# Keys and queries of four attention units turned by TensorE instead of by small transfers

## The chip, the cores and the metric

The kernel runs on one core of one Trainium2 chip. Time is device microseconds (us) of one execution on that core. Three executions of the kernel before took 579.68, 582.94 and 583.62 us; their median is 582.94 us. One more execution was taken by the hardware profiler; the rows shown here come from it.

## The reference

Three layers follow each other. Everything is float32, and the matrix products are made as sums of three products of a rounded part and a remainder, so that they keep float32's precision.

```
q, k, v: (2, 8, 768, 64)                   # batch, heads, tokens, head size
state = gamma[h] * state + k[t] v[t]^T     # retention, token by token, per head
y[t]  = q[t] state / sqrt(64)
x = y as (1536 tokens, 512)
h = x @ w_in   (512 x 2048);  g = max(h, 0) + log1p(exp(-|h|));  x = g @ w_out   (2048 x 512)
h = x @ w2_in  (512 x 2048);  g = h * clip(h + 3, 0, 6) / 6;     out = g @ w2_out (2048 x 512)
```

## The kernel before, in words

**Attention** is made in 12 units of 128 tokens (`attend(u)`), chunked: with q, k and v of a unit in SBUF, TensorE makes S (scores, from the turned `kT` and `qT`), I (scores times values), D (the unit's k-v product, added to the state `st`), and C (the carried state times `qT`). ScalarE then copies the unit's output from PSUM to `x`. Units 0 to 3 are whole units of 128 tokens; from unit 4 on (`START`) a unit is two halves of 64, and its PSUM banks are banks 2 and 3 alone (`bank_groups`): the turned keys, the turned queries, the scores and the outputs of these units take the same two banks after each other. Units 0 to 7 turn q and k on TensorE (T: 4 transposes of 128x128 each for k and for q against `ident`); ScalarE copies kT from PSUM, VectorE multiplies qT from PSUM by a table. Units 8 to 11 (`FIRST` on) fetch q and k a second time, in blocks (`kb`, `qb`: per unit 32 transfers of 16 KB, issued from SP's and POOL's queues), which VectorE's 32x32 transpose turns in SBUF.

**The first MLP layer** works on three chunks of 512 tokens, and on 16 column tiles of w_in and 16 row tiles of w_out. A G1 (`gemm1`) is 12 matmuls of 128x512 for one tile of w_in, a G2 (`gemm2`) 12 for one tile of w_out. Chunk 0 is made plainly while the attention units 4 to 11 stand in the gaps between its G1 and G2. Chunks 1 and 2 are made together: for `PLAIN` pairs of tiles plainly (4 G1 a pair over both chunks), for the other pairs (`PAIRS`) by seven products instead of eight (`early_step`, products P1 to P7 of 6 matmuls each, 42 where the plain way has 48), whose operands are sums and differences of x (`xl`) and of the words of w_in (`forms`, from words kept in DRAM as `words_in` and fetched back into `wf`). Every weight tile arrives as 64-bit words (`raw`) and is turned into float32 (`cv`) by ScalarE and VectorE (`Words.made`): ScalarE writes the low bits and the sign, then either VectorE scales and caps (two instructions) or ScalarE scales and VectorE clamps (one each, `BY_ACT`).

**The second MLP layer** works on two blocks of 768 tokens (b = 0 is block A) and 8 pairs of tiles, in 16 steps of seven products (`xf`, 128x384) and 12 sums (`w,parts`, 128x512) each. Stage 0 is block A with pairs 0 to 3, stage 1 block B with all eight pairs, stage 2 block A with pairs 4 to 7. `operands(b)` makes the seven x operands `xf` of a block from `between` (the first layer's result, which stays in SBUF) by 7 copies on ScalarE and 7 + 4 subtractions on VectorE. Those of block A are stored to DRAM (`stash_xP`) after stage 0 and fetched again for stage 2. The words of this layer are made from `late_in` and `late_out` at times that are set against the step that uses them.

**Order.** The kernel adds tasks with a cost, a due time and the buffers they take and give; `Plan.run` simulates the engines with these costs and records the instructions of all engines in the order it finds. TensorE's due times come from the written list `pe`: the attention blocks are put into it by `spread(units, start, per)`, one block each `per` GEMMs.

Of the kernel before, what the change touches and what calls it, by code (L numbers as in the profile page):

```python
# [18 lines left out]
P = 128  # L19
# [125 lines left out]
def kernel(ctx, tc, q, k, v, w1_in, w1_out, w2_in, w2_out, table, out):  # L145
# [28 lines left out]
    def BY_DVE(n):  # L174
# [2 lines left out]
    BY_DMA = ()  # L177

    def BY_ACT(n):
        return n >= 20  # L180

    def DIRECT(n):
        return True
# [62 lines left out]
    room("hi", 2, [P, CH], F32R)  # L246
    room("lo", 3, [P, CH], F32R)
    for name, n, shape, dtype in (("sums", 1, [P, 4, CH // 2], F32), ("wf", 1, [P, 2, CH], F32), ("xl", 7, [P, 2, 2, CH], F32R), ("hs", 3, [P, CH], F32), ("g2", 5, [P, CH], F32), ("hi2", 7, [P, CH], F32R), ("lo2", 7, [P, CH], F32R),
                                  ("basel", 1, [P, CH], F32), ("partl", 2, [P, CH], F32), ("totall", 1, [P, CH], F32), ("xf", 7, [P, 2, 2, QT], F32R), ("keep", START + 2, [P, CH], F32), ("tf0", 2, [P, 2, QT], F32), ("tf1", 2, [P, 2, QT], F32),
                                  ("base", 1, [P, QT], F32), ("part", 2, [P, QT], F32), ("total", 1, [P, QT], F32),  # L250
                                  ("c", 2, [P, 2, QT], F32), ("ob", 4, [P, CH], F32), ("e2", 2, [P, 2, QT], F32), ("parts", 3, [P, 2, 2, QT], F32R)):
        nc.pool(name, n)
        slots[name], kinds[name] = {}, (shape, dtype)
# [23 lines left out]
        pe += [("S", u)] + [("C", u)] * (u % (S // P) > 0) + [("D", u)] + ([("Tk", u + 1), ("Tq", u + 1)] if u + 1 < START else []) + [("I", u)]  # L277
    gaps = {}

    def spread(units, start, per):  # L280
        for n, u in enumerate(units):
            todo = ("T", "S", "I", "C")[u >= FIRST:]
            for i, block in enumerate(todo):
                gaps.setdefault(start + int((len(todo) * n + i) * per), []).extend({"T": [("Tk", u), ("Tq", u)], "I": [("I", u), ("D", u)]}.get(block, [(block, u)]))
# [251 lines left out]
    for i, key in enumerate(order):  # L536
# [3 lines left out]
    shapes = {n: [P, H, D] for n in ("q", "k", "v", "vs")}  # L540
    shapes.update({n: [P, NP, C] for n in ("kT", "qT", "pt", "kb", "qb")})
    counts = ({"q": LD, "k": LD, "v": LD, "kT": 1, "qT": 2, "vs": 2},
              {"kb": 1, "qb": 1, "k": 2, "v": 2, "kT": 1, "qT": 1, "vs": 1, "pt": 1})
# [58 lines left out]
    def attend(u):  # L602
# [37 lines left out]
        if u < START:  # L640
            at = [begin + 10 * u, begin + 10 * u + 1, begin + 10 * u + 3]
        else:
            at = [d["S" if ph else "Tk"] - 9.0 + x / 2 for x in range(3)]
        ik, iv = load("k", at[0], 2 if u == 0 else 1), load("v", at[2])
        if ph:
            ikb, iqb = (task("SP", 0.48 * 4 * (SHARE[n] + 1), blocks(n), [], d["S"] - 25.0, take=own(n), load=2.0, hold=HOLD + d["S"] - 30.0) for n in ("kb", "qb"))
        else:
            iq = load("q", at[1])
        if u == START - 1:
            for f in order[AHEAD:]:  # L650
# [17 lines left out]
        if ph:  # L668
            kt = task("DVE", TT, in_blocks("kb", "kT"), [ikb], d["S"] - 2.5, take=own("kT"), give=[("kb", u)])
            qt = task("DVE", TT, in_blocks("qb", "qT"), [iqb], d["S"] - 1.8, take=own("qT"), give=[("qb", u)])  # L670
            qt = task("DVE", TT, lambda: nc.vector.tensor_tensor(tile_of("qT"), tile_of("qT"), tq_sb, ALU.mult), [qt, ready["q"]], d["S"] - 1.1)
        else:
            tp = task("PE", cost["Tk"], turned("k"), [ik, ready.get(("o", u - 1)) if u > START else None], d["Tk"], take=[("bank", ("kP", u))])
            kt = task("ACT", ACP, lambda: nc.scalar.activation(tile_of("kT"), bank(("kP", u)), AF.Copy), [tp], d["S"] - 1.0,
                      take=own("kT"), give=[("kP", u)])
            tp = task("PE", cost["Tq"], turned("q"), [iq], d["Tq"], take=[("bank", ("qP", u))], give=[("q", u)])
# [316 lines left out]

    B_OF = {"P1": (0, 0), "P2": (1, 0), "P3": (1, 1), "P4": 4, "P5": 1, "P6": 2, "P7": 3}

    def operands(b):


        i = b * MID
        x = lambda j, k: x2(b)[:, 2 * j:2 * j + 2, k * QT:(k + 1) * QT]  # L1000
        before = T["x2", b]
        when = {name: due[name, i] - (30.0 if b == 0 else 5.0) for name in PRODUCTS}
        made = {}
        early = HOLD + due["P1", i] - 45.0 + 21.0 * b

        def tf(n):
            return at_slot((f"tf{b}", n))

        def put(n, a, c, op, after, at):
            made[n] = nc.add("DVE", dve(2 * QT), lambda: nc.vector.tensor_tensor(tf(n), a(), c(), op), after, at, take=[(f"tf{b}", (f"tf{b}", n))], hold=early)  # L1010

        put(1, lambda: x(0, 1), lambda: x(0, 0), ALU.subtract, before, when["P6"] - 2.5)
        put(2, lambda: x(1, 1), lambda: tf(1), ALU.subtract, [made[1]], when["P6"] - 1.5)
        put(3, lambda: x(1, 1), lambda: x(0, 1), ALU.subtract, before, when["P7"] - 1.5)
        put(4, lambda: x(1, 0), lambda: tf(2), ALU.subtract, [made[2]], when["P4"] - 1.5)
        users = {1: [made[2]], 2: [made[4]]}
        for n, us in users.items():
            for u in us:
                u.give.append((f"tf{b}", n))
                nc.users.setdefault((f"tf{b}", n), []).append(u)  # L1020
        for name in PRODUCTS:
            n, key = B_OF[name], ("xf", b, name)
            source = (lambda n=n: tf(n)) if isinstance(n, int) else (lambda n=n: x(*n))
            give = [(f"tf{b}", n)] if isinstance(n, int) else []
# [8 lines left out]
            c = nc.add("SP", 0.45, lambda key=key, home=home: nc.sync.dma_start(out=home, in_=at_slot(key).rearrange("p a j n -> p (a j n)").bitcast(F32)),  # L1033
                       [a, d], when[name] + 4.0, give=[key], load=2.4)
            again = "xf", 2, name
            i = len(STEPS) - (NPAIR - MID)
            T["xf", 2, name] = [nc.add("SP", 0.45, lambda key=again, home=home: nc.sync.dma_start(out=at_slot(key).rearrange("p a j n -> p (a j n)").bitcast(F32), in_=home),
                                       [c], due[name, i] - 8.0, take=[("xf", again)], load=2.4, hold=HOLD + due[name, i] - 20.0)]
# [170 lines left out]
```

## Time and profile before

| | |
|---|---|
| median of three executions | 582.94 us (579.68 to 583.62) |
| profiled execution, its own time | 581.4 us |
| its span in the profile | 579.6 us |
| TensorE (PE) busy | 561.5 us |
| VectorE (DVE) busy | 430.4 us |
| ScalarE (ACT) busy | 358.0 us |
| GpSimd (POOL) busy | 33.7 us |
| moved by DMA | 112.60 MB |
| granted TensorE clock | 1.00 in every stretch |

The span is what the profile's rows cover; the profiled execution's own time is 1.8 us longer, and 1.5 us below the median of the other three. Matmuls are pipelined, so a row's duration is longer than the distance to the next matmul's start.

### The profile page before, as it was taken

The page shows a single profiled execution, that of the slowest core. Times are in us where ns is not written, and L with a number is a line of the kernel's source. Part 1 is how long each engine was busy: PE and PEld are TensorE (multiplying, and loading weights), DVE is VectorE, ACT ScalarE, POOL GpSimd, SP SyncE. Part 2 cuts the span into 40 slices and gives each one's busy share as a digit, 9 for nine tenths or more (in the row PEclk, how much of TensorE's full clock was granted, in tenths as well). Part 3 has the DMA queues.
Part 4 walks back from the last instruction along what each step waited for, and adds up shares of the span by engine and source line. Part 5 has one row for each costly group of instructions (what it writes and reads, how often), then busy time and mean ns, then how long its engine had stood idle before and what let it go on. Part 6 is the DMA issues. An engine that isn't in the chain of part 4 may idle for free.

```text
span 579.6 us, 9697 instructions
## 1 busy us (share of the span) xinstructions
PE 561.5 (97%) x3667; PEld 476.6 (82%) x3667; DVE 430.4 (74%) x768; ACT 358.0 (62%) x578; POOL 33.7 (6%) x61
## 2 busy tenths in 40 slices
PE   8999999899899999999999999999999999999997
PEld 7777887677688888887888888888888989888995
DVE  4999997886796786979996678754988884445434
ACT  3589969888494546476974774538779862232220
POOL 0000532423000000000000000000000000000000
PEclk9999999999999999999999999999999999999999
DMA  9999796967862316199899351152746742955003
GB/s 198 232 292 290 218 251 138 314 169 207 271 246 77 105 72 220 72 297 323 299 414 329 134 182 37 42 163 103 284 158 235 285 146 81 379 203 190 1 1 110
DMA packets 91088, 112.60 MB, mean 194 GB/s; under 512 B 49312, under 2 KB 66720, under 8 KB 91040
## 3 DMA queue, kind: packets, MB, share of 16 engines
q1 hardware_dynamic: 88784, 109.87, 58.2%
q0 software_dynamic: 2256, 2.10, 1.8%
q8 instruction: 29, 0.48, 0.3%
q14 instruction: 19, 0.16, 0.1%
HBM read 82.06 MB, written 28.57 MB: 191 GB/s over the span
## 4 chain that ended last, share of the span: by engine, by line
PE 75%; DMA 9%; ACT 7%; DVE 5%; issue 1%; SPq 1%; DVEq 0%; POOL 0%; ACTq 0%; POOLq 0%
PE banks L45 75%; DMA raw<-in_moe_w_out_dram 4%; ACT cv L45 2%; DMA stash_out<-raw 1%; DMA kb<-in_k_dram 1%; ACT raw L45 1%; ACT w L45 1%; SPq L45 1%; DMA stash_h<-hs 1%; DMA g<-stash_h 1%; DVE raw L45 1%; DMA qb<-in_q_dram 1%; DVE cv L45 1%; ACT e L45 1%; ACT parts L45 1%
## 5 line engine op out<-in xcount | busy, mean ns | idle before, releaser
L45 PE MATMUL banks<-w,parts 128*128 128x512 f32 x579 | 137.0, 390 | 0.0
L45 PE MATMUL banks<-xf,w 128*128 128x384 f32 x672 | 125.4, 338 | 2.4 <-ACT base L45 1.5
L45 PEld LDWEIGHTS banks<-w,parts 128*128 128x128 f32 x579 | 108.0, 188 | 21.2
L45 PE MATMUL banks<-hi,w 128*128 128x512 f32 x384 | 125.2, 393 | 0.0
L45 PEld LDWEIGHTS banks<-xf,w 128*128 128x128 f32 x672 | 117.8, 188 | 8.3 <-ACT base L45 2.7
L45 PEld LDWEIGHTS banks<-hi,w 128*128 128x128 f32 x384 | 72.1, 188 | 15.3
L45 PE MATMUL banks<-xl,w 128*128 128x512 f32 x348 | 82.5, 391 | 0.4 <-DVE hs L45 0.4
L45 PEld LDWEIGHTS banks<-xl,w 128*128 128x128 f32 x348 | 64.9, 188 | 14.7 <-DVE hs L45 0.8
L45 PE MATMUL banks<-lo,w 128*128 128x512 f32 x192 | 75.0, 391 | 0.9 <-DVE lo L45 0.9
L45 ACT ACTIVATE e<-c,three 128x384 f32<-128x384 f32 (+1 forms) x32 | 24.6, 770 | 54.4 <-DVE c L45 54.1
L45 ACT ACTIVATE cv<-raw,half 128x512 uint32<-128x512 uint32 x64 | 48.3, 755 | 9.2 <-DMA raw<-in_moe_w_in_dram 4.3
L45 ACT ACTIVATE cv<-raw 128x512 f16<-128x512 int32 x64 | 50.6, 790 | 1.4
L45 DVE TENSOR_SCALAR raw<-raw 128x512 f32<-128x512 f32 x84 | 35.7, 426 | 15.6 <-ACT raw L45 13.2
L45 DVE SCALAR_TENSOR_TENSOR cv<-raw,cv 128x512 uint32<-128x512 uint32 x64 | 44.2, 690 | 1.5
L45 PE MATMUL banks<-x_hi,w 128*128 128x512 f32 x128 | 42.9, 401 | 2.1 <-ACT g L45 1.3
L45 ACT ACTIVATE hi<-g 128x512 fp32r<-128x512 f32 x48 | 30.0, 627 | 21.1 <-DVE g L45 12.4
L45 PEld LDWEIGHTS banks<-lo,w 128*128 128x128 f32 x192 | 36.1, 188 | 8.5 <-DVE lo L45 1.2
L45 DVE TENSOR_TENSOR parts<-c,parts 128x768 fp32r<-128x768 f32 x32 | 30.6, 957 | 14.2 <-ACT parts L45 13.9
L45 ACT ACTIVATE e<-e 128x512 f32<-128x512 f32 x48 | 29.6, 627 | 18.2 <-DVE e L45 18.0
L45 DVE TENSOR_TENSOR lo<-g,hi 128x512 fp32r<-128x512 f32 x48 | 32.9, 687 | 8.1 <-ACT hi L45 7.4
L45 ACT ACTIVATE parts<-c 128x768 fp32r<-128x768 f32 x32 | 27.0, 844 | 17.3 <-DVE c L45 17.2
L45 DVE TENSOR_TENSOR c<-total,banks 128x384 f32<-128x384 f32 x16 | 8.8, 553 | 36.1 <-PE banks L45 36.0
(102 smaller groups left out, 689.5 us busy)
## 6 DMA issues: line engine op xcount, KB each, us to landing
raw<-in_moe_w_in_dram SPq DMA_DIRECT2D x32, 512.0 KB, 5.4
raw<-in_moe_w_out_dram SPq DMA_DIRECT2D x32, 512.0 KB, 6.1
w<-stash_out SPq DMA_DIRECT2D x32, 512.0 KB, 5.3
w<-parts_out SPq DMA_DIRECT2D x16, 512.0 KB, 7.1
stash_out<-raw SPq DMA_DIRECT2D x16, 512.0 KB, 3.0
stash_xP<-xf SPq DMA_DIRECT2D x7, 768.0 KB, 7.0
xf<-stash_xP SPq DMA_DIRECT2D x7, 768.0 KB, 8.4
parts_out<-w SPq DMA_DIRECT2D x8, 512.0 KB, 6.4
```

The costliest lines, as they stand in the source:

```text
L45: return self.plan.tc.keep_in_program_order(getattr(self.engine, op)(*args, **kwargs))
```

## The change

Units 8 to 11 no longer fetch q and k in blocks: they turn q and k on TensorE as units 4 to 7 do (`TURNED = 'kq'`), with kT copied by ScalarE and qT multiplied from PSUM by VectorE. Their blocks are spread one each 1.2 GEMMs instead of 1.5, with T in front. `PLAIN` goes from 2 to 1, so chunks 1 and 2 have seven pairs made by products and one plain. `BY_ACT` starts at tile 16 instead of 20, so four more tiles of the first layer are scaled by ScalarE. Block A's operands of stage 2 are made again from `between` (`operands(stage)` for three stages) instead of stored and fetched. The due times of the second layer's words are 4 us later, their fetches may start 8 us earlier.

```
-    PLAIN = 2
+    PLAIN = 1
+    TURNED = 'kq'
     def BY_ACT(n):
-        return n >= 20
+        return n >= 16
...
+    def turns(u):
+        return "kq" if u < FIRST else TURNED
     def spread(units, start, per):
         for n, u in enumerate(units):
-            todo = ("T", "S", "I", "C")[u >= FIRST:]
+            todo = ("T", "S", "I", "C")[not turns(u):]
...
-    spread(range(FIRST, NU), 18, 1.5)
+    spread(range(FIRST, NU), 18, 1.2)
...  in late_out
-        at = due["P1", USED[f // 2]] - (40 - 2.0 * f if f < 2 * MID else 20)
-        t = x.made(at, at - 10.0, 1.45, [], hold=(HOLD + at - 24) * (f >= 2 * MID))
+        at = due["P1", USED[f // 2]] - (40 - 2.0 * f if f < 2 * MID else 16)
+        t = x.made(at, at - 10.0, 1.45, [], hold=(HOLD + at - 36) * (f >= 2 * MID))
...  in late_in
-        at = due["P1", USED[p]] - (20 if p else 12)
+        at = due["P1", USED[p]] - (16 if p else 12)
...  in attend
         if ph:
-            ikb, iqb = (task("SP", 0.48 * 4 * (SHARE[n] + 1), blocks(n), [], ...) for n in ("kb", "qb"))
-        else:
+            ib = {n[0]: task(...) for n in ("kb", "qb") if n[0] not in TURNED}
+        if "q" in turns(u):
             iq = load("q", at[1])
...
-            kt = task("DVE", TT, in_blocks("kb", "kT"), [ikb], d["S"] - 2.5, take=own("kT"), give=[("kb", u)])
-            qt = task("DVE", TT, in_blocks("qb", "qT"), [iqb], d["S"] - 1.8, take=own("qT"), give=[("qb", u)])
-            qt = task("DVE", TT, lambda: nc.vector.tensor_tensor(tile_of("qT"), tile_of("qT"), tq_sb, ALU.mult), ...)
...  now for units 8 to 11 too:
             tp = task("PE", cost["Tk"], turned("k"), [ik, ready.get(("o", u - 1)) if u > START else None], ..., take=[("bank", ("kP", u))])
             kt = task("ACT", ACP, lambda: nc.scalar.activation(tile_of("kT"), bank(("kP", u)), AF.Copy), [tp], ...)
+            tp = task("PE", cost["Tq"], turned("q"), [iq, ready.get(("o", u - 1)) if u >= FIRST else None], ..., take=[("bank", ("qP", u))], give=[("q", u)])
             qt = task("DVE", PSX, lambda: nc.vector.tensor_tensor(tile_of("qT"), bank(("qP", u)), tq_sb, ALU.mult), ...)
...
-    def operands(b):
-        i = b * MID
+    def operands(stage):
+        i, b = STAGE.index(stage), stage % 2
...
-            T["xf", b, name] = [a, d]
-            if b:
-                continue
-            home = kept(f"stash_x{name}", 4 * QT)
-            ...  store of xf to home, and its fetch for stage 2
+            T["xf", stage, name] = [a, d]
...
-    for b in range(2):
-        operands(b)
+    for stage in range(3):
+        operands(stage)
```

How the instructions move is shown at three places. The first is TensorE at unit 11, the last one: `ident,k` and `ident,q` are the transposes, `qT,kT` is S, `pt,vs` is I, `vs,k` is D, `xl` rows are a plain G1 of chunk 1, `hi` and `lo` rows belong to a G2. Before:

```order
L45 MATMUL banks<-hi_95,w_1786 128x512
L45 MATMUL banks<-qT_0_151,kT_0_150 64x64 x16
L45 MATMUL banks<-xl_1373,w_1461 128x512 x6
L45 MATMUL banks<-xl_1377,w_1461 128x512 x6
L45 MATMUL banks<-pt_0_153,vs_0_152 64x64 x16
L45 MATMUL banks<-vs_0_152,k_1_147 64x64 x8
L45 MATMUL banks<-hi_96,w_89 128x512
```

and now:

```order
L45 MATMUL banks<-hi_95,w_88 128x512
L45 MATMUL banks<-ident,k_1_149 128x128 x4
L45 MATMUL banks<-ident,q_1_147 128x128 x4
L45 MATMUL banks<-xl_1631,w_1530 128x512 x6
L45 MATMUL banks<-xl_1651,w_1530 128x512 x6
L45 MATMUL banks<-qT_0_153,kT_0_152 64x64 x16
L45 MATMUL banks<-hi_96,w_1368 128x512
```

The transposes stand one GEMM ahead of S. The same holds at units 8 to 10.

The second place is ScalarE from unit 8's output copy (`x_190<-banks`) to unit 9's kT copy in the changed kernel; `cv` and `raw` rows make words of the first layer, `g`, `e`, `hi` belong to the activation:

```order
L45 ACTIVATE hi_95<-g_93 128x512
L45 ACTIVATE raw_0_69<-raw_0_69 128x512
L45 ACTIVATE x_190<-banks 128x2x4x64
L45 ACTIVATE cv_1_75<-raw_1_70,half 128x512
L45 ACTIVATE w_1416<-cv_3_77 128x512
L45 ACTIVATE cv_1_75<-raw_1_70 128x512
L45 ACTIVATE raw_1_70<-raw_1_70 128x512
L45 ACTIVATE g_92<-banks 128x512
L45 ACTIVATE kT_0_152<-banks 128x512
L45 ACTIVATE e_90<-e_90 128x512
```

The kT copy is new there; five instructions stand between it and the output copy, which frees the banks that the transposes take.

The third place is VectorE at unit 9 before, where a transpose of a block (`kT<-kb`) stands among the first layer's work:

```order
L45 TENSOR_SCALAR raw_1_70<-raw_1_70 128x512
L45 SCALAR_TENSOR_TENSOR cv_3_77<-raw_1_70,cv_3_77 128x512
L45 TENSOR_SCALAR e_91<-g_93 128x512
L45 TENSOR_TENSOR w_82<-cv_3_77,w_82 128x512
L45 STREAM_TRANSPOSE kT_0_150<-kb_0_144 128x512
L45 TENSOR_TENSOR pt_0_153<-banks,small 128x2x4x64
L45 TENSOR_SCALAR raw_2_71<-raw_2_71 128x512
```

and now:

```order
L45 TENSOR_TENSOR w_1416<-cv_3_77,w_1416 128x512
L45 TENSOR_SCALAR raw_1_70<-raw_1_70 128x512
L45 TENSOR_TENSOR qT_0_153<-banks,tq_sb 128x512
L45 SCALAR_TENSOR_TENSOR cv_1_75<-raw_1_70,cv_1_75 128x512
L45 SCALAR_TENSOR_TENSOR g_94<-g_94,e_90 128x512
```

No instruction of VectorE waits for a block transfer any more; one multiplication from PSUM is left of three instructions.

## Rows read from the trace of the kernel before

**Rows 1.** The page, section 1: busy us, share of the span, instructions.
```profile
PE 561.5 (97%) x3667; PEld 476.6 (82%) x3667; DVE 430.4 (74%) x768; ACT 358.0 (62%) x578; POOL 33.7 (6%) x61
```
**Rows 2.** Windows: stretch, length, busy PE, PEld, DVE, ACT, POOL, clock, DMA, GB/s.
```profile
32.00:100.00 68.00, 68.00 (x749) 54.37 (x740) 62.89 (x124) 60.63 (x101) 16.97 (x27) 1.00 0.85 235
100.00:151.00 51.00, 44.07 (x532) 34.06 (x528) 40.20 (x73) 39.72 (x66) 15.69 (x26) 1.00 0.79 221
151.00:260.00 109.00, 109.00 (x562) 89.61 (x552) 85.42 (x152) 66.18 (x109) 0.00 (x0) 1.00 0.50 171
260.00:310.00 50.00, 49.63 (x219) 40.66 (x218) 48.88 (x87) 38.95 (x69) 0.00 (x0) 1.00 0.92 339
...
400.00:450.00 50.00, 48.76 (x241) 43.03 (x240) 41.44 (x76) 41.15 (x67) 0.00 (x0) 1.00 0.59 208
...
490.00:580.00 90.00, 85.44 (x426) 76.49 (x424) 38.34 (x60) 22.52 (x33) 0.00 (x0) 1.00 0.41 150
```
**Rows 3.** Timeline, PE, 100 to 151: start, us, instructions, [idle before, releaser].
```profile
105.39 0.68 PE L45 MATMUL banks<-qT,st 64*64 64x64 f32 x16 [0.98 <-DVE st L45]
106.33 0.68 PE L45 MATMUL banks<-qT,st 64*64 64x64 f32 x16 [0.25 <-DVE st L45]
...
113.41 0.69 PE L45 MATMUL banks<-qT,kT 64*64 64x64 f32 x32 [0.71 <-DVE qT L45]
...
123.74 1.15 PE L45 MATMUL banks<-qT,st 64*64 64x64 f32 x32
...
129.17 0.50 PE L45 MATMUL banks<-x_hi,w 128*128 128x512 f32 x1 [1.33 <-ACT g L45]
...
136.96 0.73 PE L45 MATMUL banks<-x_hi,w 128*128 128x512 f32 x2 [0.75 <-DMA w<-cv]
...
143.50 1.15 PE L45 MATMUL banks<-qT,st 64*64 64x64 f32 x32
...
146.01 0.50 PE L45 MATMUL banks<-lo,w 128*128 128x512 f32 x1 [0.93 <-DVE lo L45]
...
150.50 0.69 PE L45 MATMUL banks<-qT,kT 64*64 64x64 f32 x32 [1.71 <-DVE qT L45]
```
**Rows 4.** Timeline, DVE, unit 11's keys.
```profile
144.67 0.71 DVE L45 STREAM_TRANSPOSE kT<-kb 128x512 f32<-128x512 f32 x1 [3.05 <-DMA qb<-in_q_dram]
```
**Rows 5.** Timeline, PE, unit 5's transposes between a G2 and a G1.
```profile
43.08 0.60 PE L45 MATMUL banks<-ident,k 128*128 128x128 f32 x4
43.51 0.60 PE L45 MATMUL banks<-ident,q 128*128 128x128 f32 x4
43.87 0.48 PE L45 MATMUL banks<-x_hi,w 128*128 128x512 f32 x1
...
46.69 0.39 PE L45 MATMUL banks<-hi,w 128*128 128x512 f32 x1
```
**Rows 6.** Timeline, PE, a run of products of chunks 1 and 2.
```profile
183.84 16.48 PE L45 MATMUL banks<-xl,w 128*128 128x512 f32 x72
```
**Rows 7.** Timeline, ACT, the output copies of units 8, 9 and 10.
```profile
109.53 0.58 ACT L45 ACTIVATE x<-banks 128x512 f32<-128x512 f32 x1
...
127.54 0.58 ACT L45 ACTIVATE x<-banks 128x512 f32<-128x512 f32 x1
...
147.93 0.58 ACT L45 ACTIVATE x<-banks 128x512 f32<-128x512 f32 x1
```
**Rows 8.** Groups by form: count, busy us, mean ns of one, idle before.
```profile
L45 DVE TENSOR_TENSOR w<-sums,w 128x512 fp32r<-128x512 f32 x28 | 18.4, 685 | 0.7 <-ACT w L45 0.7
...
L45 DVE TENSOR_TENSOR xf<-tf,xf 128x768 fp32r<-128x768 f32 x8 | 7.6, 953 | 0.3 <-ACT xf L45 0.3
...
L45 ACT ACTIVATE xf<-tf 128x768 fp32r<-128x768 f32 x8 | 6.7, 840 | 5.3 <-PE banks L45 4.2 <-DVE tf L45 0.8
...
L45 DVE TENSOR_TENSOR sums<-wf 128x256 f32<-128x256 f32 x12 | 4.7, 420 | 2.5 <-DMA wf<-words_in 2.5
```
**Rows 9.** Timeline, PE, hand-over from stage 0 to stage 1.
```profile
363.55 2.41 PE L45 MATMUL banks<-xf,w 128*128 128x384 f32 x12 [0.27 <-ACT base L45]
```

More of the change, by code (lines that the diff above doesn't have):

```diff
@@ L278 @@
     gaps = {}
+    def turns(u):
+        return "kq" if u < FIRST else TURNED
     def spread(units, start, per):
         for n, u in enumerate(units):
-            todo = ("T", "S", "I", "C")[u >= FIRST:]
+            todo = ("T", "S", "I", "C")[not turns(u):]
             for i, block in enumerate(todo):
-                gaps.setdefault(start + int((len(todo) * n + i) * per), []).extend({"T": [("Tk", u), ("Tq", u)], "I": [("I", u), ("D", u)]}.get(block, [(block, u)]))
+                gaps.setdefault(start + int((len(todo) * n + i) * per), []).extend({"T": [("T" + n, u) for n in turns(u)], "I": [("I", u), ("D", u)]}.get(block, [(block, u)]))
     spread(range(START, FIRST), 0, 1.2)
-    spread(range(FIRST, NU), 18, 1.5)
+    spread(range(FIRST, NU), 18, 1.2)
     n = 0
@@ L467, in late_in @@
         x = [Words(1, (1, 0, 2 * p + f), words[1][0]) for f in range(2)]
-        at = due["P1", USED[p]] - (20 if p else 12)
-        t = [v.made(at + 2 * f, at - 10.0 + f, 1.75, [v.raw_k], hold=(HOLD + at - 24) * (p >= MID)) for f, v in enumerate(x)]
+        at = due["P1", USED[p]] - (16 if p else 12)
+        t = [v.made(at + 2 * f, at - 10.0 + f, 1.75, [v.raw_k], hold=(HOLD + at - 36) * (p >= MID)) for f, v in enumerate(x)]
         forms(1, p, lambda f: x[f].w().bitcast(F32), t, [v.cv_k for v in x], at)
@@ L542 @@
     counts = ({"q": LD, "k": LD, "v": LD, "kT": 1, "qT": 2, "vs": 2},
[L543 removed]
+              {"q": 2, "k": 2, "v": 2, "kT": 1, "qT": 1, "vs": 1, "pt": 1})
     for n, m in counts[0].items():
@@ L642, in attend @@
         else:
-            at = [d["S" if ph else "Tk"] - 9.0 + x / 2 for x in range(3)]
+            at = [d["T" + turns(u)[0] if turns(u) else "S"] - 9.0 + x / 2 for x in range(3)]
         ik, iv = load("k", at[0], 2 if u == 0 else 1), load("v", at[2])
         if ph:
-            ikb, iqb = (task("SP", 0.48 * 4 * (SHARE[n] + 1), blocks(n), [], d["S"] - 25.0, take=own(n), load=2.0, hold=HOLD + d["S"] - 30.0) for n in ("kb", "qb"))
-        else:
+            ib = {n[0]: task("SP", 0.75 * 4 * (SHARE[n] + 1), blocks(n), [], d["S"] - 25.0, take=own(n), load=2.0, hold=HOLD + d["S"] - 30.0) for n in ("kb", "qb") if n[0] not in TURNED}
+        if "q" in turns(u):
             iq = load("q", at[1])
@@ L667, in attend @@
         sc, ds, o = ([(n, j, u) for j in range(2)] for n in ("sc", "ds", "o"))
-        if ph:
-            kt = task("DVE", TT, in_blocks("kb", "kT"), [ikb], d["S"] - 2.5, take=own("kT"), give=[("kb", u)])
-            qt = task("DVE", TT, in_blocks("qb", "qT"), [iqb], d["S"] - 1.8, take=own("qT"), give=[("qb", u)])
-            qt = task("DVE", TT, lambda: nc.vector.tensor_tensor(tile_of("qT"), tile_of("qT"), tq_sb, ALU.mult), [qt, ready["q"]], d["S"] - 1.1)
+        if "k" not in turns(u):
+            kt = task("DVE", TT, in_blocks("kb", "kT"), [ib["k"]], d["S"] - 2.5, take=own("kT"), give=[("kb", u)])
         else:
@@ L675, in attend @@
                       take=own("kT"), give=[("kP", u)])
-            tp = task("PE", cost["Tq"], turned("q"), [iq], d["Tq"], take=[("bank", ("qP", u))], give=[("q", u)])
+        if "q" not in turns(u):
+            qt = task("DVE", TT, in_blocks("qb", "qT"), [ib["q"]], d["S"] - 1.8, take=own("qT"), give=[("qb", u)])
+            qt = task("DVE", TT, lambda: nc.vector.tensor_tensor(tile_of("qT"), tile_of("qT"), tq_sb, ALU.mult), [qt, ready["q"]], d["S"] - 1.1)
+        else:
+            tp = task("PE", cost["Tq"], turned("q"), [iq, ready.get(("o", u - 1)) if u >= FIRST else None], d["Tq"], take=[("bank", ("qP", u))], give=[("q", u)])
             qt = task("DVE", PSX, lambda: nc.vector.tensor_tensor(tile_of("qT"), bank(("qP", u)), tq_sb, ALU.mult), [tp, ready["q"]],
@@ L994 @@
     B_OF = {"P1": (0, 0), "P2": (1, 0), "P3": (1, 1), "P4": 4, "P5": 1, "P6": 2, "P7": 3}
-    def operands(b):
-        i = b * MID
+    def operands(stage):
+        i, b = STAGE.index(stage), stage % 2
         x = lambda j, k: x2(b)[:, 2 * j:2 * j + 2, k * QT:(k + 1) * QT]
         before = T["x2", b]
-        when = {name: due[name, i] - (30.0 if b == 0 else 5.0) for name in PRODUCTS}
+        when = {name: due[name, i] - (5.0 if stage else 30.0) for name in PRODUCTS}
         made = {}
-        early = HOLD + due["P1", i] - 45.0 + 21.0 * b
+        early = HOLD + due["P1", i] - (24.0 if stage else 45.0)
         def tf(n):
-            return at_slot((f"tf{b}", n))
+            return at_slot((f"tf{stage}", n))
         def put(n, a, c, op, after, at):
-            made[n] = nc.add("DVE", dve(2 * QT), lambda: nc.vector.tensor_tensor(tf(n), a(), c(), op), after, at, take=[(f"tf{b}", (f"tf{b}", n))], hold=early)
+            made[n] = nc.add("DVE", dve(2 * QT), lambda: nc.vector.tensor_tensor(tf(n), a(), c(), op), after, at, take=[(f"tf{stage}", (f"tf{stage}", n))], hold=early)
         put(1, lambda: x(0, 1), lambda: x(0, 0), ALU.subtract, before, when["P6"] - 2.5)
@@ L1018, in operands @@
             for u in us:
-                u.give.append((f"tf{b}", n))
-                nc.users.setdefault((f"tf{b}", n), []).append(u)
+                u.give.append((f"tf{stage}", n))
+                nc.users.setdefault((f"tf{stage}", n), []).append(u)
         for name in PRODUCTS:
-            n, key = B_OF[name], ("xf", b, name)
+            n, key = B_OF[name], ("xf", stage, name)
             source = (lambda n=n: tf(n)) if isinstance(n, int) else (lambda n=n: x(*n))
-            give = [(f"tf{b}", n)] if isinstance(n, int) else []
+            give = [(f"tf{stage}", n)] if isinstance(n, int) else []
             a = nc.add("ACT", act(2 * QT), lambda key=key, source=source: nc.scalar.activation(at_slot(key)[:, 0], source(), AF.Copy),
@@ L1028, in operands @@
                 at_slot(key)[:, 1], source(), at_slot(key)[:, 0].bitcast(F32), ALU.subtract), [a], when[name] + 0.9, give=give)
-            T["xf", b, name] = [a, d]
-            if b:
-                continue
-            home = kept(f"stash_x{name}", 4 * QT)
[L1033 to L1038, printed above, removed]
+            T["xf", stage, name] = [a, d]
     def step(i):
```

2 lines of the change are left out of this document (1 added, 1 removed).

## Prediction, made before the changed kernel ran

> **What bounds the kernel.** I read the engine table first, then the stretches, then the timeline of TensorE. TensorE is busy 561.5 of 579.6 us [rows 1], at full clock in every stretch shown [rows 2]. So the time is TensorE's work plus its waits, and only 18.1 us are not work. Most of that is at the two ends or in one place: from 100 to 151 us it works 44.07 of 51.00 us, 6.93 us idle [rows 2]. From 32 to 100 and from 151 to 260 it never stops; 400 to 450 loses 1.24 us, and most of the 4.56 us lost after 490 are the end, when the last tile is scaled and stored. The changed attention units 8 to 11 stand in the stretch from 100 to 151, so the reader should see there who keeps TensorE waiting. The timeline names it [rows 3]: S of units 9 and 11 waits for qT, 0.71 and 1.71 us; C of unit 8 waits for the state, 0.98 and 0.25 us; a G2 waits for `lo`, 0.93 us; one G1 for a bank that ScalarE frees late, 1.33 us; another for weights that POOL's queue brings, 0.75 us. These make 6.66 of the 6.93 us.
>
> Behind several of them is one thing. VectorE works in order, and its transpose of unit 11's keys sat 3.05 us until a block had landed [rows 4]; `lo` at 146.01 and qT at 150.50 stood behind it. The same engine makes the words that ScalarE needs next.
>
> **TensorE's own work.** Unit 5 shows what turning costs: its 8 transposes begin at 43.08 and the next GEMM at 43.87, so 0.79 us; that GEMM takes 2.82 us to the next one's start [rows 5], where 12 matmuls in a run take 12 x 0.2266 = 2.72 us (16.48 us less the last one's overlap of 0.39, over 71 steps [rows 6]). So 0.89 us a unit, and 4 x 0.89 = **+3.56 us**. The lower bound is 4 x 0.79 = 3.16. The Trainium skill, in "VectorE: DVE Perf Modes", section "The three transpose paths", gives 390 ns for a 128x128 transpose on TensorE (in bf16) and 311 ns for VectorE's 32x32 blocks. By that figure, an estimate, 32 transposes would cost 12.5 us of the binding engine. The trace speaks against that sum: eight in 0.79 us.
>
> The seventh pair made by products takes 42 matmuls instead of 48: 6 x 0.2266 = **-1.36 us**. The 14 transfers of `stash_xP` never kept TensorE waiting in a row here, so taking them away is worth nothing by itself.
>
> **The waits in 100 to 151.** The two qT waits and `lo` go with the blocks: 3.35 us. C of unit 8 came right behind D; now a GEMM of 2.72 us stands between, more than its 1.23 us: gone for units 8 to 10, and unit 11 keeps six matmuls, 1.36 us. The remaining 2.35 us hang on ScalarE and POOL. POOL issued 48 of the block transfers, and ScalarE was late because words were late; I count these as gone too: **-6.93 us**. If they stay, it is -4.58.
>
> New waits can come, since all these units share PSUM banks 2 and 3. T of unit 9 cannot begin until unit 8's output has been copied out, and S waits for the new kT copy (0.59 us, four of them) on ScalarE. In the trace the output copies of units 8, 9 and 10 end at 110.11, 128.12 and 148.51 [rows 7], and their C ended at 107.01, 124.89 and 144.65 [rows 3]: 3.10, 3.23 and 3.86 us later. The GEMM between C and the next T covers 2.72. Were ScalarE as late again, T would wait 0.38 + 0.51 + 1.14 = 2.03 us, and S behind kT as much for four units, 2.41 us: 4.4 us together, the upper end. The lower end is 0: units 4 to 7 are laid out in this way from 32 to 100, with ScalarE busy 60.63 of 68 us (89%), and TensorE never waited [rows 2]. With four kT copies ScalarE would have 39.72 + 2.4 = 42.1 us of work in some 48: the same 88%. So I stay near the lower row, **+1.5 us**; above 0, because the last unit's blocks stand close to each other ahead of chunk 0's end, and the three late copies show that ScalarE's queue here is not always ready when C ends.
>
> **VectorE and ScalarE elsewhere.** Tiles 16 to 19 move some 2.7 us to ScalarE and 1.7 us off VectorE before 100, where TensorE does not wait: 0. If that cover went, it would be at most 2.7 us.
>
> The seventh pair costs VectorE four sums at 0.42 us, four remainders (three at 0.685, one short at 0.42) and five combinations at 0.685 [rows 8]: 7.6 us, between 151 and 310. From 151 to 260 VectorE is busy 85.42 of 109 us; there they fit. From 260 to 310 it is busy 48.88 of 50 [rows 2], and there 6.5 us of them would become waits. The pair's own work lies before 260 by its place in TensorE's list, so 0, with 6.5 as the upper end.
>
> Stage 2 gets 7 copies at 0.84 us on ScalarE and 11 subtractions at 0.953 us on VectorE [rows 8]: 5.9 and 10.5 us, in a stretch (490 to 580) where the two are busy 22.52 and 38.34 of 90 us [rows 2]. The hand-over from stage 0 to stage 1 makes the same operands with the same slots and cost TensorE 0.27 us [rows 9]: **+0.27**, at most 1. The later due times and earlier fetches of the second layer's words act on the 1.24 us between 400 and 450: 0, between -1.24 and +1.24.
>
> **Sum**: -6.93 + 1.5 + 3.56 - 1.36 + 0.27 = -2.96 us. The profiled execution took 581.4 us, so it would take 578.4. The median of the three executions is 1.5 us above it, and the changed kernel will be measured by such a median: 582.94 - 2.96 = **580.0 us**.
>
> **Rivals.**
>
> *All waits go and none comes.* -6.93 + 3.16 - 1.36 - 1.24 = -6.4 us: 576.5. For it: 32 to 100 shows no wait with the same layout. Against it: it needs every small term at its best end. 13 in 100.
>
> *ScalarE stays late.* The G1's and the weights' waits remain, and T and kT wait 4.4 us: -4.58 + 4.4 + 3.56 - 1.36 + 0.27 = +2.3 us: 585.2. It decides once the output copy ends more than 2.72 us after C. For it: it was past that three times out of three. Against: VectorE's waits for blocks, which made the words late, are gone. The Trainium skill says in "Perfetto Trace Analysis", section "Matmuls", that independent groups should rotate through different PSUM banks so that one's evacuation overlaps the next one's matmuls; this change sends more groups through the same two banks. 20 in 100.
>
> *Slower: VectorE becomes the bound.* The 7.6 us of the seventh pair push the first layer's last softplus and the second layer's words behind 260, where VectorE has 1.12 us free. TensorE then waits 6.5 us around 260 to 330: -2.96 + 6.5 = +3.5 us: 586.5. It decides when the work left over at 260 is more than the free 1.12 us. Against it: 23.6 us are free just before. 9 in 100.
>
> *Both of these.* +2.3 + 6.5 = +8.8 us: 591.7. 6 in 100.
>
> *Transposes do not overlap.* One alone takes 0.28 us (0.60 us for four, less three steps of 0.43 / 4 [rows 5]); were the 32 made singly, TensorE would work 32 x 0.28 = 9.0 us instead of 3.56: +5.4 us, 585.4. The same rows exclude nearly all of it: 2 in 100. The skill's figure named above would add 8.9 us instead.
>
> My forecast has the remaining 50 in 100, its own range being 577 to 582.5.
>
> **Numbers.** The range must hold 8 in 10: it takes the forecast, the best case and the late ScalarE, from 575.5 (the best case, 1 us for the scatter of a median) to 586.0. One per cent, 5.8 us, is about what a measurement of this kernel can tell, with executions 3.9 us apart. Faster by more than that, under 577.1, needs the best case or a bit of luck on top of the forecast: 0.15. Slower, over 588.8, is the two rivals together, and what else I have not seen: 0.08. Within: 0.77.
>
> **What would show it.** In the changed profile TensorE should be busy some 2 us longer in all, with about 2 us idle in the stretch of units 8 to 11, waiting for ScalarE's `x` or `kT` if for anything. VectorE should show no wait for `q` or `k`, and POOL almost no work. If ScalarE is late, rows of `ident,k` will carry idle time released by `x`. If VectorE binds, idle time will stand between 260 and 330, released by `lo`, `c` or `between`. At stage 2 the first products should wait less than 1 us. I am wrong if the waits before 151 vanish and the time does not fall: then a later stretch gave it back, and its waits must be longer than before.

## The result, and the profile after

The changed kernel took 573.16 us (median of four executions, 572.33 to 573.40), the kernel before 583.28 us beside it. The ratio is 0.9871, with a 95% interval of 0.9825 to 0.9917: some 1.3% faster. The quotient of the two medians is lower, 0.983: the four executions of the kernel before spread from 579.68 to 584.20 us, and beside the later runs its medians were 580.54 to 581.18. The forecast was 580.0 with a range of 575.5 to 586.0, so the direction was right, the size too small, and the time lies 2.3 us below the range. "Within 1%" had 77 of 100 chances; the ratio lies outside it, and so does the whole interval of the second measurement (e5 below, 0.9837 to 0.9891).

The profiled execution took 572.94 us with a span of 571.2, where before it was 581.4 and 579.6. The forecast sum was -2.96; these executions differ by -8.46. So 5.5 us have to be explained. The rest of the 6.8 us between 580.0 and 573.16 is the 1.5 us that the forecast added because the median before lay above the profiled execution; the changed kernel's median lies 0.2 us above its own. One execution of e1 below, of 1972.37 us, is left out of its ratio.

The page of the changed kernel, section 1, answers to [rows 1]:

```profile
PE 561.3 (98%) x3693; PEld 477.7 (84%) x3693; DVE 439.7 (77%) x780; ACT 365.3 (64%) x595; POOL 5.7 (1%) x13
```

POOL is nearly free, as foreseen. TensorE was to be busy some 2 us longer and is not: 561.3 against 561.5, with 26 more instructions. That is a first hint that "busy" before held time that was not work.

Windows of the changed kernel (columns as in [rows 2]):

```profile
100.00:151.00 51.00, 51.00 (x589) 40.89 (x579) 41.97 (x79) 42.25 (x73) 1.88 (x2) 1.00 0.83 248
151.00:260.00 109.00, 109.00 (x550) 89.74 (x549) 91.81 (x164) 67.79 (x114) 0.00 (x0) 1.00 0.44 147
260.00:310.00 50.00, 50.00 (x225) 41.68 (x224) 48.26 (x87) 38.70 (x69) 0.00 (x0) 1.00 0.71 247
```

From 100 to 310 TensorE has no idle row at all. All 6.93 us of the stretch from 100 to 151 went, no new wait came, and VectorE at 48.26 of 50 us does not hold anybody up. All that TensorE still waits for in a visible row is this (waits of the changed kernel, PE: total us, times, longest):

```profile
PE banks L45 <- ACT w L45: 1.6, 2, 1.1
PE banks L45 <- POOL ident masks.py:199: 1.5, 1, 1.5
PE banks L45 <- DVE qT L45: 1.0, 1, 1.0
PE banks L45 <- ACT base L45: 0.5, 2, 0.3
PE banks L45 <- DVE c L45: 0.3, 1, 0.3
PE banks L45 <- DMA q<-in_q_dram: 0.2, 1, 0.2
PE banks L45 <- DVE part L45: 0.2, 1, 0.2
```

The first three and `q` lie before 32 us, where the kernel starts; the others lie in the second layer.

**Where the time came from.** The second MLP layer has 16 steps, numbered here from 0. The order inside a step can differ, but from step 1 on the same matmuls stand ahead of a step's start in both kernels, so these starts are clean marks. Steps 1, 10, 11 and 12 of the kernel before (timeline, PE; `xf` rows begin a step; columns as in [rows 3]):

```profile
329.01 4.71 PE L45 MATMUL banks<-xf,w 128*128 128x384 f32 x24 [0.55 <-ACT between L45]
...
473.56 4.35 PE L45 MATMUL banks<-xf,w 128*128 128x384 f32 x24
...
489.14 4.35 PE L45 MATMUL banks<-xf,w 128*128 128x384 f32 x24
...
504.72 4.36 PE L45 MATMUL banks<-xf,w 128*128 128x384 f32 x24
```

and of the changed kernel steps 1, 10, 11, a later row of step 11, and steps 12 and 13:

```profile
320.85 4.37 PE L45 MATMUL banks<-xf,w 128*128 128x384 f32 x24
...
463.88 4.69 PE L45 MATMUL banks<-xf,w 128*128 128x384 f32 x24
...
479.80 2.27 PE L45 MATMUL banks<-xf,w 128*128 128x384 f32 x12
482.34 2.41 PE L45 MATMUL banks<-xf,w 128*128 128x384 f32 x12 [0.27 <-ACT base L45]
...
495.98 4.78 PE L45 MATMUL banks<-xf,w 128*128 128x384 f32 x24
...
511.99 4.35 PE L45 MATMUL banks<-xf,w 128*128 128x384 f32 x24
```

The changed kernel is 8.16 us ahead at step 1, 9.68 at step 10, 8.74 at step 12, and 8.4 at the end of the span. The forecast for these stretches was -3.23 up to step 1 (-6.93 + 1.5 + 3.56 - 1.36), 0 from there to step 10, and +0.27 behind it. Nearly all of the miss is ahead of step 1; 1.5 us more lie in steps 1 to 10, and the hand-over to stage 2 takes about one back.

How far one profile can be read shows in e9 below, which has the instructions of the kernel before up to 150 us. Its S of unit 11 starts at 149.63 us and that of the kernel before at 150.50, so some 0.9 us of the 8.16 can be scatter.

### The profile page after: what moved, and what is told of

Read it like the earlier page. It is cut to its first block, busy times and chain, and to the rows that moved or that the text cites. A ratio compares the mean times of both kernels' runs of the same rounds, so it can differ in the third digit from the quotient of the medians.

```text
span 571.2 us, 9550 instructions
## 1 busy us (share of the span) xinstructions
PE 561.3 (98%) x3693; PEld 477.7 (84%) x3693; DVE 439.7 (77%) x780; ACT 365.3 (64%) x595; POOL 5.7 (1%) x13
## 4 chain that ended last, share of the span: by engine, by line
PE 79%; ACT 7%; DVE 7%; DMA 5%; issue 1%; SPq 0%; DVEq 0%; ACTq 0%
PE banks L45 79%; ACT cv L45 3%; DMA raw<-in_moe_w_in_dram 3%; DVE c L45 1%; ACT e L45 1%; DVE cv L45 1%; DVE parts L45 1%; DMA raw<-in_moe_w_out_dram 1%; ACT parts L45 1%; ACT raw L45 1%; DVE xf L45 1%; DVE raw L45 1%; DMA q<-in_q_dram 1%; ACT xf L45 1%; DVE w L45 0%
## 5 line engine op out<-in xcount | busy, mean ns | idle before, releaser
L45 PE MATMUL banks<-xl,w 128*128 128x512 f32 x342 | 80.8, 391 | 0.0
L45 DVE TENSOR_SCALAR raw<-raw 128x512 f32<-128x512 f32 x80 | 33.6, 424 | 13.0 <-ACT raw L45 12.8
L45 DVE SCALAR_TENSOR_TENSOR g<-g,e 128x512 f32<-128x512 f32 x48 | 32.6, 686 | 3.6 <-ACT e L45 3.5
```

Of the source, the lines that this page charges most:

```text
L45: return self.plan.tc.keep_in_program_order(getattr(self.engine, op)(*args, **kwargs))
```

## The experiments

The first theory (A) was that leaving out the block transfers is the whole gain, and that the other edits do nothing. Its rivals gave a share to each of the others. When the first runs had shown that the blocks alone gain nothing in the end, a second theory (D) took its place: the blocks' gain is real but is given back in the second layer, whose words are placed by the old due times, and the new times are what keeps it. Its rival (E) is that the two are separate losses, each with a gain of its own. Each kernel ran in five rounds beside the kernel before. Ratios are to that kernel, with 95% intervals.

| run | edit | median us | ratio to before |
|---|---|---|---|
| e1_turned_only | before, units 8 to 11 turned | 579.94 | 0.9989 (0.9972 to 1.0006) |
| e2_turned_15 | the same, a block each 1.5 GEMMs | 578.28 | 0.9970 (0.9954 to 0.9987) |
| e9_late_alone | before, new due times alone | 578.88 | 0.9987 (0.9964 to 1.0010) |
| e7_turned_late | before, turned and new due times | 574.70 | 0.9884 (0.9861 to 0.9908) |
| e5_changed_again | the changed kernel | 572.95 | 0.9864 (0.9837 to 0.9891) |
| e6_late_times_old | changed, old due times | 575.50 | 0.9906 (0.9879 to 0.9934) |
| e3_plain2 | changed, two plain pairs | 576.29 | 0.9927 (0.9902 to 0.9952) |
| e8_act20 | changed, `BY_ACT` from 20 | 572.96 | 0.9857 (0.9833 to 0.9882) |
| e4_stash_back | changed, operands stored and fetched | 571.88 | 0.9861 (0.9833 to 0.9889) |
| e11_stash_again | the same once more | 571.92 | 0.9867 (0.9845 to 0.9890) |
| e12_stash_15 | the same, a block each 1.5 GEMMs | 574.14 | 0.9911 (0.9888 to 0.9934) |
| e10_turned_twice | changed, every transpose of units 8 to 11 twice | 576.99 | 0.9945 (0.9925 to 0.9964) |

### Only the turning (e1)

```
 kernel before
+    TURNED = 'kq'
-    spread(range(FIRST, NU), 18, 1.5)
+    spread(range(FIRST, NU), 18, 1.2)
     + turns(u), the T blocks, kT on ScalarE and qT on VectorE from PSUM, as in the change
```

> The kernel before with one part of the change: units 8 to 11 turned by TensorE, blocks 1.2 GEMMs apart. Theory A (the block transfers made the waits of 100 to 151 us): the 6.9 us of waits there go, TensorE works about 2.8 us more for the transposes (0.70 us a unit, as the changed kernel's trace has it), nothing later changes: 3.5 to 4.5 us faster than before, ratio about 0.993. Theory B (the order of the blocks matters, not who turns): the same here, but most of it lost again in the run with 1.5 GEMMs between. Theory C (the four tiles that ScalarE scales made room on VectorE): waits of 3 us or more stay between 100 and 151, ratio 0.997 or above.

Measured: 579.94 us, ratio 0.9989, not separable from no change. Yet up to the second layer theory A held: TensorE works 51.00 of 51.00 us from 100 to 151, and step 1 starts at 324.86, 4.15 us earlier than before (4.8 with the three sums of this step that were already made by then). At step 10 it starts at 471.37 against 473.56, only 2.19 earlier, and at step 12 it is 503.58 against 504.72. The gain was given back inside the second layer. PE's timeline of this run there, with the starts of steps 8, 9, 10 and 11:

```profile
437.52 2.27 PE L45 MATMUL banks<-xf,w 128*128 128x384 f32 x12
...
453.92 4.37 PE L45 MATMUL banks<-xf,w 128*128 128x384 f32 x24
...
466.10 1.31 PE L45 MATMUL banks<-xf,w 128*128 128x384 f32 x6 [1.57 <-DVE c L45]
...
471.37 3.71 PE L45 MATMUL banks<-xf,w 128*128 128x384 f32 x18
...
488.00 4.36 PE L45 MATMUL banks<-xf,w 128*128 128x384 f32 x24
```

An undisturbed step takes 15.58 us (before, 489.14 to 504.72). These three take 16.40, 17.45 and 16.63; in the kernel before they took 16.05, 15.81 and 15.58. So 3.0 us of the lead went here. The row of 466.10 names `c`, an instruction of VectorE. The timeline of VectorE in this run shows why `c` was late:

```profile
464.08 0.43 DVE L45 TENSOR_SCALAR raw<-raw 128x512 f32<-128x512 f32 x1 [4.12 <-ACT raw L45]
...
465.50 0.55 DVE L45 TENSOR_TENSOR c<-total,banks 128x384 f32<-128x384 f32 x1
```

`c` needed nothing from `raw`; it stood behind it on the same engine, which had waited 4.12 us. The chain of waits of this run (start, us, what) goes on to what `raw` waited for:

```profile
449.22 7.86 DMA stash_out<-raw
...
457.11 4.84 DMA raw<-in_moe_w_out_dram
...
461.96 0.77 ACT cv L45
...
...
466.10 6.51 PE banks L45 x30
```

A buffer of `raw` was being stored for 7.86 us, and only then the next words could be fetched into it, 4.84 us. From 449 to 457 us the DMA engines were 96% busy. TensorE came earlier, the words did not.

### The turning with the new due times (e7), the due times alone (e9), and the change without them (e6)

e7 is e1 with this; e9 is the kernel before with this alone; e6 takes it back from the changed kernel:

```
-        at = due["P1", USED[f // 2]] - (40 - 2.0 * f if f < 2 * MID else 20)
-        t = x.made(..., hold=(HOLD + at - 24) * (f >= 2 * MID))
+        at = due["P1", USED[f // 2]] - (40 - 2.0 * f if f < 2 * MID else 16)
+        t = x.made(..., hold=(HOLD + at - 36) * (f >= 2 * MID))
-        at = due["P1", USED[p]] - (20 if p else 12)
+        at = due["P1", USED[p]] - (16 if p else 12)
         and hold at - 24 to at - 36 there too
```

The earlier fetch, and the later time of the output words, hold for pairs 4 to 7 alone; these are first used in steps 8 to 11.

> The kernel before with units 8 to 11 turned by TensorE and the new times of the second layer's words, nothing else. Theory D: the 3.7 us that turning alone had gained at the start of step 4 now last to the end: 3.5 to 5 us faster than before, ratio 0.992 to 0.994, where turning alone was 0.9989. Rival: under 1.5 us faster, ratio 0.997 or above, and the waits between 440 and 480 us are as with turning alone.

> The changed kernel with the old due times and fetch times of the second layer's words. Theory D (the gain of the early stretch was given back at the second layer's words, between 440 and 480 us, and the new times kept it): the waits on `c`, `part` and `base` of 1.5 to 2.7 us come back there, 1.5 to 3 us slower than the changed kernel. Rival (the new times are worth nothing; PLAIN and the four tiles scaled by ScalarE kept it): within 0.7 us of it.

> The kernel before with the new times of the second layer's words alone; the block transfers stay. Theory E (two separate losses: 6.9 us of waits at the attention units, and some 5 us in steps 0 to 9 of the second layer, most of it pauses too short to show as idle): the second goes, 3 to 5 us faster, ratio 0.992 to 0.995, and the waits between 100 and 151 us are as before. Rival (the times only keep what turning gained, they are worth nothing without it): within 1 us of before.

Measured: the two edits together give 0.9884 where the turning alone gave 0.9989 and the times alone 0.9987. The intervals of the last two include no change; the first is a gain of 6.5 us, more than the 3.5 to 5 expected. Taking the times back from the changed kernel costs 2.55 us (575.50 against 572.95 beside it). So the two edits make more together than the sum of both, as theory D has it. In e7 step 1 starts at 324.24, within 0.62 us of e1 (0.1 with equal work done), and then (timeline, PE, steps 9, 10 and 11):

```profile
450.03 4.71 PE L45 MATMUL banks<-xf,w 128*128 128x384 f32 x24
...
466.13 4.36 PE L45 MATMUL banks<-xf,w 128*128 128x384 f32 x24
...
481.71 4.35 PE L45 MATMUL banks<-xf,w 128*128 128x384 f32 x24
```

The rows carry no idle time, and the two steps take 16.10 and 15.58 us. VectorE's wait for `raw` there is 1.67 us instead of 4.12, and the store that was the slow one in e1 is issued at 443.7 us instead of 449.22, while TensorE begins step 9 only 3.9 us earlier. In e6 the old wait is back, further on (timeline, PE):

```profile
474.69 3.39 PE L45 MATMUL banks<-xf,w 128*128 128x384 f32 x18 [1.95 <-DVE c L45]
```

The edit has two halves, a later due time and an earlier earliest fetch. Which of them does it was not tried; the earlier store in e7 speaks for the fetch.

Theory E is not all wrong. The kernel before itself lost time in steps 7 to 9: from 424.77 to 473.56 are 48.79 us, where three undisturbed steps take 46.79. In e9 that loss is gone (timeline, PE, steps 7 and 10):

```profile
423.77 4.36 PE L45 MATMUL banks<-xf,w 128*128 128x384 f32 x24
...
470.56 4.69 PE L45 MATMUL banks<-xf,w 128*128 128x384 f32 x24
```

These three steps take 46.79 us, and TensorE still idles 6.85 us between 100 and 151. The spans of the profiles are 579.6 before, 578.7 in e1, 577.0 in e9 and 572.4 in e7. By them the times alone gain 2.6 us, the turning alone 0.9 and both 7.2, so 3.7 come only together. Over the executions the 2.6 us are not borne out: the interval of e9's ratio allows a gain of 2.1 us at most (0.9964).

### Two plain pairs instead of one (e3)

```
-    PLAIN = 1
+    PLAIN = 2
```

> The changed kernel with two plain pairs instead of one. TensorE has six matmuls more, 6 x 0.227 = 1.4 us, and VectorE 7.6 us less between 151 and 310. Theory: TensorE binds and VectorE's work is covered, so 1.4 us slower than the changed kernel. Rival: VectorE's work was not quite covered, then the same or up to 1 us faster than it.

Measured: 576.29 us, 3.1 to 3.3 us more than the changed kernel, where six matmuls were forecast, 1.36 us. In the profile step 1 starts at 324.58, 3.73 us later than in the changed kernel. PE's timeline of this run shows a wait there that the changed kernel has not:

```profile
259.66 2.88 PE L45 MATMUL banks<-xl,w 128*128 128x512 f32 x12
263.54 1.66 PE L45 MATMUL banks<-xl,w 128*128 128x512 f32 x6 [1.00 <-DVE hs L45]
```

`hs` is a sum of the products' results on VectorE. The expectation had 1.4 us, and its rival less. The two starts are 3.88 us apart where twelve free matmuls take 2.72, so 1.16 were lost, and the row behind is 0.13 longer than six free matmuls (1.66 against 5 x 0.227 + 0.39): 1.29 and not 1.00. With 1.36 that is 2.65 us; another 0.56 lies before 32 us (31.34 against 30.78 at the same wait for `w`), where the edit changes nothing. The remaining 0.5 us are not explained. By step 8 of the second layer the distance is down to 2.5 us (434.96 against 432.50), and the spans differ by 2.4. A wait for `hs` of 0.2 to 1.5 us stands in the profiles of before, e1, e2, e3, e7 and e9, which have two plain pairs, and in none with one.

### ScalarE's share of the words (e8)

```
-        return n >= 16
+        return n >= 20
```

> The changed kernel with ScalarE scaling from tile 20 on, as before. Theory: TensorE did not wait where these tiles are made, so 0 +- 0.5 us against the changed kernel. Rival: VectorE, 90% busy from 32 to 150 us, comes out of that stretch later by up to 1.7 us, and the time is 1 to 2 us longer.

Measured: 572.96 us, the changed kernel 572.95 beside it. The edit shows no effect in either direction, as forecast.

### Block A's operands stored and fetched again (e4, e11), and the spacing (e2, e12)

```
 changed kernel, e4 and e11
-    for stage in range(3):
-        operands(stage)
+    for b in range(2):
+        operands(b)        # with stash_xP stored after stage 0 and fetched for stage 2
 e12, on top of it; e2 the same on top of e1
-    spread(range(FIRST, NU), 18, 1.2)
+    spread(range(FIRST, NU), 18, 1.5)
```

> The changed kernel with block A's operands stored after stage 0 and fetched for stage 2 again, as before (14 transfers of 768 KB). Theory: the transfers lie beside TensorE's work, so 0 to 0.3 us faster (the 0.27 us wait at the hand-over to stage 2 goes). Rival: they delay the second layer's words, and the waits of the kernel before between 320 and 450 us (2.3 us in all) come back: 1 to 2 us slower.

> The changed kernel with block A's operands stored and fetched, once more, against the medians of 572.95 and 573.16 us that the changed kernel had. Theory F (making the operands again costs TensorE 1 to 2 us around the start of stage 2, by operands that come just too late): 571 to 572.3 us. Rival (no difference): 572.7 to 573.5.

Measured: 571.88 and 571.92 us. Against 573.16 and 572.95 this is 1.0 to 1.3 us less, where e4's expectation had 0 to 0.3, but the ratios to the kernel before, 0.9861 and 0.9867 beside 0.9871 and 0.9864, don't separate the versions. The rows do, at the hand-over. PE's timeline of e4, steps 10 and 13 (463.04 and 509.83):

```profile
463.04 4.37 PE L45 MATMUL banks<-xf,w 128*128 128x384 f32 x24
...
509.83 4.37 PE L45 MATMUL banks<-xf,w 128*128 128x384 f32 x24
```

These three steps take 46.79 us, and 46.79 in e11 as well; in the changed kernel they take 48.11 (463.88 to 511.99), in its second profile 47.87. Making the operands again costs TensorE 1.1 to 1.3 us there, although the only idle row shows 0.27. It is the fastest version in the table, but its total is not proven better: the profiles of e4 and e11, the same kernel, have spans of 569.6 and 571.4 us.

> As the run before it, but the blocks of units 8 to 11 stand 1.5 GEMMs apart instead of 1.2, so some stand right behind each other. Theory A: within 1 us of it, since the waits came from the transfers. Theory B: C waits for the state again and S for kT at units where no GEMM stands between, 2 to 5 us slower than with 1.2.

> As the run before it, with the blocks of units 8 to 11 1.5 GEMMs apart. With turning alone 1.5 was 1.7 us faster than 1.2, in steps 8 to 10 of the second layer, where the old times of the words lost time. If that was a real gain of the spacing: 1 to 2 us faster than the run before it. If it was only less loss at the words: within 0.7 us of it.

Measured: on the turning alone a spacing of 1.5 was 1.7 us faster than 1.2 by medians, with overlapping intervals and spans of 578.7 us in both profiles; on the changed kernel with the stash it was 2.2 us slower, which neither side of the expectation had. So there is no gain in the spacing itself, and theory B's 2 to 5 us of loss did not show with the turning alone. In e12 TensorE waits where the second layer begins (timeline, PE; step 1):

```profile
324.57 3.74 PE L45 MATMUL banks<-xf,w 128*128 128x384 f32 x20 [0.71 <-ACT between L45]
```

That start is 2.9 us later than in e11 (321.64), 1.4 of it because six sums of the step were already made. But by step 10 only 0.5 us are left (465.31 against 464.81), and the spans differ by 0.5 as well. So the profiles do not show where the 2.2 us of the medians come from; this stays open.

### Every transpose twice (e10)

```
-                for p in range(NP):
+                for p in [*range(NP)] * (2 if u >= FIRST else 1):
```

> The changed kernel with each transpose of units 8 to 11 made twice, into the same place: 32 transposes more on TensorE, nothing else moved. By the changed kernel's trace (8 transposes in about 0.75 us, the GEMM behind them 0.1 longer once) 2.7 to 3.2 us slower than the changed kernel. By the prediction's 0.89 us a unit: 3.56. If some of it stands in front of a wait for ScalarE that is already there: under 2. If each took the 0.28 us of one alone: 9.0.

Measured: 576.99 us. PE's timeline of this run at unit 11, keys, queries and C:

```profile
146.99 1.03 PE L45 MATMUL banks<-ident,k 128*128 128x128 f32 x8
147.86 1.04 PE L45 MATMUL banks<-ident,q 128*128 128x128 f32 x8
...
157.81 1.15 PE L45 MATMUL banks<-qT,st 64*64 64x64 f32 x32
```

The same C starts at 154.23 in the changed kernel, 3.58 us earlier. Of these, 0.09 lie ahead of the first transpose of unit 8 (95.89 against 95.80), so 32 more transposes cost 3.49 us, 0.109 us each. The expectation had 2.7 to 3.2. In the whole time they cost 3.8 to 4.0 us by medians and 2.8 by the profiled spans.

## Why the prediction was right or wrong

The direction was right, and the waits that were to go went. Three steps of the sum failed. The second layer's words were put at 0, where the new times are worth 2.55 us: this is a mechanism that the prediction did not have. The cost of the waits was read from idle time, some 1.5 us too small. And new waits for ScalarE were put at 1.5 us and did not come.

**Transposes, +3.56: right.** In the changed kernel the transposes of unit 9 begin at 111.05 and the next GEMM at 111.84: 0.79 us, and the same at units 8, 10 and 11. e10 gives 3.49 us for 32 more. The figure of 390 ns for one (in bf16) in the Trainium skill ("VectorE: DVE Perf Modes", "The three transpose paths") is 3.6 times what a transpose costs in this queue; a sum of 12.5 us would have called the change a loss.

**The waits in 100 to 151, -6.93: right in what goes, short in what it is worth.** All eight went. But a visible wait costs more than its row. These are the neighbours of the G1 that waited 1.33 us in [rows 3], at 129.17 (timeline, PE, kernel before):

```profile
127.45 0.39 PE L45 MATMUL banks<-hi,w 128*128 128x512 f32 x1
...
129.51 0.40 PE L45 MATMUL banks<-x_lo,w 128*128 128x512 f32 x1
```

A free matmul starts 0.23 us after the one ahead, while its row lasts 0.39. From 127.45 to 129.17 are 1.72 us, so 1.49 were lost; and the first step behind the wait took 0.34 instead of 0.23. That makes 1.60 us lost where the row says 1.33. By the same reading of starts the waits for `w`, `lo` and `hs` cost 0.26 more than their rows, those at the attention blocks I, C and S 0.06 to 0.07, and the second wait of C 0.22: some 1.5 us over nine waits. The prediction took the idle column for the loss.

One reading of a cause was wrong. S of unit 9 waited 0.71 us for qT, but no block held qT back there. It stood behind `raw`, which waited for ScalarE (timeline, DVE, kernel before):

```profile
111.51 0.43 DVE L45 TENSOR_SCALAR raw<-raw 128x512 f32<-128x512 f32 x1 [1.35 <-ACT raw L45]
```

Why this wait went too is not shown. In e9, with the same instructions there, TensorE idles 6.85 us in this stretch, but otherwise shared out: 2.30 of it before one G1.

**New waits for ScalarE, +1.5: this did not happen.** The timeline of ScalarE in the changed kernel, with the output copies of units 8, 9 and 10:

```profile
108.31 0.60 ACT L45 ACTIVATE x<-banks 128x512 f32<-128x512 f32 x1 [0.44 <-PE banks L45]
...
123.56 0.60 ACT L45 ACTIVATE x<-banks 128x512 f32<-128x512 f32 x1
...
141.53 0.60 ACT L45 ACTIVATE x<-banks 128x512 f32<-128x512 f32 x1 [0.49 <-PE banks L45]
```

and TensorE's C blocks, with the T that comes next after the first and the third:

```profile
107.11 1.15 PE L45 MATMUL banks<-qT,st 64*64 64x64 f32 x32
...
111.05 0.60 PE L45 MATMUL banks<-ident,k 128*128 128x128 f32 x4
...
122.36 1.15 PE L45 MATMUL banks<-qT,st 64*64 64x64 f32 x32
...
140.34 1.15 PE L45 MATMUL banks<-qT,st 64*64 64x64 f32 x32
...
144.28 0.60 PE L45 MATMUL banks<-ident,k 128*128 128x128 f32 x4
```

The copies end 0.65, 0.65 and 0.64 us behind C, where before it was 3.10, 3.23 and 3.86. For units 8 and 10 ScalarE even waited for C. T comes 2.1 us after the copy at both places shown, so sharing two banks cost nothing here. The prediction carried the late copies of before over as if they belonged to ScalarE's load; with the block transfers gone they were early at nearly the same load (42.25 of 51 us). That VectorE's waits for blocks were the cause is argued from [rows 4], not shown by a run that changes them alone.

**The seventh pair, -1.36: too small.** e3 gives 3.1 to 3.3 us by medians. The pair took out the wait for `hs` as well. Its work on VectorE hid, as said: no idle row from 151 to 310.

**Due times and fetches of the second layer's words, 0 with 1.24 either way: the step whose mechanism was missing.** It is worth 2.55 us in the changed kernel (e6), and 5 to 6 on the turning (579.94 in e1, 574.70 in e7; by the two ratios 1.05%). The prediction read only the idle time before the change, 1.24 us between 400 and 450, where the starts of steps 7 to 9 show a loss of 2.0. It did not ask what a TensorE that arrives 4 us earlier meets in the second layer. Its own closing sentence named the symptom (a later stretch gives the gain back), but gave it no price. The 5.5 us of the miss do not contain these 2.55: the forecast expected no loss there, and the new times prevented one. In e6 the kernel is as far ahead at step 10 (463.58) as the changed one and then loses 2.9 us in that step alone (18.46 us).

**Hand-over, +0.27: too small by about one.** The neighbouring stage change had shown 0.27 as an idle row, and the same row appears; the step starts say 1.1 to 1.3. By starts the neighbouring change had cost about as much in the kernel before: two of its steps took 16.18 and 16.01 us (361.01 to 377.19 to 393.21), as steps 11 and 12 of the changed kernel do. **`BY_ACT`, 0: right.**

**The account.** Up to step 1 the miss is 4.93 us. New waits that did not come make 1.5; the hidden part of the waits 1.5; the waits for `hs` (0.37) and `between` (0.55), which are gone, 0.92, and at least 0.16 hidden in the latter; and the start, where unit 4's S came at 30.78 instead of 31.53, 0.75. That is 4.8, so the stretch closes to 0.1, closer than the scatter of a profile allows to claim. The start is not the change's doing as far as the rows show: the same S moved between 30.77 and 31.40 from one experiment to another, and in e9, with the instructions of the kernel before, it came at 30.91. Steps 1 to 10 add 1.5: the kernel before lost 2.0 in steps 7 to 9, and the changed kernel less. The hand-over takes back about one.

## What to carry to other kernels

Read what a wait costs from the distance of starts around it, against the same work undisturbed, and not from the idle column. When a change makes an early stretch faster, follow the later one as if everything in it came due that much sooner: fetches and buffers that were just in time are then late, and the gain goes back unless their times move with it. And test edits in pairs, not only alone: here two whose ratios could not be told from 1 apart made 1.2% together.

## What the runs showed of the hardware

TensorE's busy time is not its work. The page of e1 and the page of e7 count the same 3699 matmuls:

```profile
PE 565.4 (98%) x3699; PEld 479.2 (83%) x3699; DVE 427.2 (74%) x760; ACT 356.7 (62%) x582; POOL 5.6 (1%) x13
```

```profile
PE 561.8 (98%) x3699; PEld 479.4 (84%) x3699; DVE 426.2 (74%) x760; ACT 355.5 (62%) x582; POOL 5.6 (1%) x13
```

The first is e1, the second e7: the same work, 3.6 us apart in busy time. Pauses of up to 0.16 us between matmuls (0.39 less 0.23) lie inside the rows. And a buffer's store and refill can be slow: 7.86 and 4.84 us in the chain of e1, where the median of this store is 3.1 us and the DMA engines were 96% busy. There the buffer that came free late held VectorE for 4.12 us and TensorE for 1.57.
